# Linear attention and a spectral mix on one core: constants loaded in sixteen pieces, two weight loads cut into row ranges

## The chip, the cores and the metric

The kernel runs on one core of one Trainium2 chip. The metric is device time of one execution in microseconds (us), lower is better. The engines are named as in the profile: PE is TensorE's matmul side and PEld its weight load, DVE is VectorE, ACT is ScalarE, POOL is GpSimd, SP is SyncE. PE, DVE and ACT compute; POOL and SP issue transfers here. Sixteen DMA engines move the data for all of them.

## The reference

```python
# q, k, v: (8, 8, 576, 64) float32: batch, heads, sequence, head width
phi = lambda x: np.where(x > 0, x, np.exp(x) - 1.0) + 1.0
q_p, k_p = phi(q), phi(k)
kv  = einsum('bhsd,bhse->bhde', k_p, v);  z = sum(k_p, axis=2)
num = einsum('bhsd,bhde->bhse', q_p, kv); den = einsum('bhsd,bhd->bhs', q_p, z) + 1e-6
x = (num / den) as (8, 576, 512)          # batch, sequence, heads * width

# w_r, w_i: (64, 512, 512) float32, one complex matrix per mode; w_ch: (512, 512)
X = rfft(x, axis=1)                       # the first 64 modes are used
Y[:, m] = X[:, m] @ (w_r[m] + 1j * w_i[m])   for m < 64, else 0
u = x + irfft(Y, n=576, axis=1)
out = u + maximum(u @ w_ch, 0)            # (8, 576, 512) float32
```

The 64 pairs of matrices w_r and w_i hold 134 MB in float32, and every byte is used once.

## The kernel before

The work has three stages. In the first (to about 112 us) the attention is computed batch by batch, and its first 64 Fourier modes are formed by matmuls with constant cosines and sines (fwd_sb). In the second (to about 388 us) the modes are multiplied by their matrices, two modes at a time: a "pair" p covers modes 2p and 2p + 1, and there are 32 pairs. While they stream, the attention rows are formed a second time, the inverse transform of the modes that are already done is folded into them, and the product with w_ch is made; a plan of work slots spreads this over the pairs. In the third stage the last modes are added and the rows are stored.

The weights of a pair are one tile of 128 partitions by 16 x 512 values in bf16. POOL loads it in two transfers, "half" 0 from w_r into the even partitions and half 1 from w_i into the odd ones (`w_load`, L117). Each transfer has 64 rows of 32 KB in float32 in the source, which arrive as rows of 16 KB in bf16: the transfer converts. Pairs 0 and 1 have a buffer each, pairs 2 to 4 three buffers of their own, and from pair 5 on two buffers are used in turn, so that the load of pair p can be issued when the product of pair p - 2 is finished. The last pair (31) is loaded in smaller pieces by `w_load_last` (L129). Before the stream, POOL also loads w_ch and the small selection constant pick_sb.

`mode_pair(p)` waits for both halves, makes 16 matmuls (`product`, L432), copies the result out of PSUM (`evacuate`, L447 and L449), does the work of its first slot, picks the rows out (`picks`, L455), does its second slot, and runs a number of matmuls that fill time (`keep_warm`, L419). All of these stand in the order written: `pin` keeps every engine's program order, and POOL's transfers among themselves too.

The constants of the inverse transform, inv_sb, are 128 partitions (64 modes, cosine and sine) by 576 values of 2 bytes, 144 KB. SP loads them in one transfer (L541) once the space that they take has been given up by the first stage. They are read first by `row_set` (L628), which makes permuted copies of them in a work slot, and later by the matmuls that add the inverse transform (L683, L745, L752, L760, L893). After inv_sb SP issues nothing until the third stage, in which it sends a copy within the chip (YZ_all, L947) and the stores of the output (L816, L822). The last product of the second stage is y_last (L513), which follows the last pieces of pair 31 one by one.

Completion of transfers is counted in eight counters for POOL's and eight for SP's, used in turn; a transfer whose counter is still in use by the one eight before it waits for that one.

Of the kernel before, what the change touches and what calls it, by code (L numbers as in the profile page):

```python
# [43 lines left out]
def kernel(  # L44
# [10 lines left out]
    nc = tc.nc  # L55
# [3 lines left out]
    NM = moe_w_r.shape[0]  # L59
# [3 lines left out]
    NDW = 4 * NDC  # L63
# [10 lines left out]
    inv_dr = nc.inline_tensor(inv_np, name="dft_inv")  # L74
# [31 lines left out]
    pin = tc.keep_in_program_order  # L106
    PIECES = (slice(0, 2), slice(2, 4), slice(4, 6), slice(6, 7), slice(7, 8))
    HALVES = [slice(0, 64), slice(64, 128)]

    LAST = NM // 2 - 1  # L110

    def w_load(p: int, half: int, pool, tag: str, bufs: int):
        if half == 0:
            w_in[p] = pool.tile([128, NDW, D], BF16, tag=tag, bufs=bufs, name=f"w{p}")
        two = (moe_w_r, moe_w_i)[half][2 * p : 2 * p + 2]
        pin(
            nc.gpsimd.dma_start(  # L117
                out=w_in[p][half::2], in_=two.rearrange("g (r dc) e -> (g r) dc e", dc=NDW)
            )
        )  # L120

    def w_load_last(pool, tag: str, bufs: int):
        w_in[LAST] = pool.tile([128, NDW, D], BF16, tag=tag, bufs=bufs, name=f"w{LAST}")
        for g in range(2):
            for half in range(2):
                rows_in = (moe_w_r, moe_w_i)[half][NM - 2 + g].rearrange("(p dc) e -> p dc e", dc=NDL)
                for dcs in PIECES if (g, half) == (1, 1) else (slice(0, NDL),):
                    dst = w_in[LAST][half::2, g * NDL + dcs.start : g * NDL + dcs.stop]
                    pin(nc.gpsimd.dma_start(out=dst, in_=rows_in[:, dcs, :]))  # L129
# [16 lines left out]
    def w_next():  # L146
        p, half = pending.pop(0)
        pool, tag, bufs = (wpool, "w", W_KEEP) if p < n_keep else (wpre, "wp", W_PRE)
        w_load(p, half, pool, tag, bufs)
# [258 lines left out]
    def w_get(p: int):  # L408
        if p not in w_in and p == LAST:
            w_load_last(wpool, "w", W_KEEP)  # L410
        elif p not in w_in:
            for half in range(2):
                w_load(p, half, wpool, "w", W_KEEP)
        return w_in[p]
# [14 lines left out]
    def product(P, x, n: int, w, dc: int, n_dc: int):  # L429
        c = dc % NDC * 32  # L430
        pin(
            nc.tensor.matmul(  # L432
                P[c : c + n, :], x, w[:, dc, :],
                start=(dc < NDC), stop=(dc >= n_dc - NDC), tile_position=(0, c),
                skip_group_check=True,
            )
        )

    def set_diagonal(p: int):
        for h in range(2):  # L440
            src = xt_v[HALVES[h], :, :, :, p].rearrange("p c t b -> p c (t b)")
            pin(nc.vector.tensor_copy(out=xz[p % 2][HALVES[h], :, h, :], in_=src))  # L442
# [19 lines left out]
    def mode_pair(p: int):  # L462
# [5 lines left out]
        for dc in range(NDW):  # L468
            product(P, xz[p % 2][:, dc].rearrange("p h n -> p (h n)"), 32, w, dc, NDW)
        if p + 1 < LAST:  # L470
            set_diagonal(p + 1)
# [15 lines left out]
    def last_pair():  # L487
        xl = ystage.tile([128, NDL, 2 * B], BF16, name="xl")
        for h in range(2):
            src = xt_v[:, (2 * h + 1) * NDC : (2 * h + 2) * NDC, :, :, LAST]  # L490
            pin(
# [3 lines left out]
            )  # L495
        w = w_get(LAST)
        kk = NM - 2
# [39 lines left out]
    inv_sb = ystage.tile([2 * NM, S], F16, name="inv_sb")  # L537
    inv2_sb = ystage.tile([128, S], F16, name="inv2_sb")
    N_LEAD = 2
    lead_sb = [ystage.tile([128, S], F16, name=f"lead{b}_sb") for b in range(N_LEAD)]  # L540
    nc.sync.dma_start(out=inv_sb, in_=inv_dr.ap())  # L541
    YE_T = ystage.tile([128, NDC, NF, 2 * B], F16, name="YE_T")
    YL = [ystage.tile([128, NDC // 2, 2, 2 * NL, NF // NL, B], F16, name="YL0")]
    Y8 = ystage.tile([128, NDC, NL, 2 * B], F16, name="Y8")
# [44 lines left out]
    def x_of(t: int):  # L589
        if t < B * NJJ:  # L590
            return x_main[t // NJJ][:, t % NJJ, :]
        i = t - B * NJJ
        return x_tail[i // 2][:, i % 2, :]
# [352 lines left out]
    for h, eng in enumerate((nc.sync, nc.gpsimd)):  # L946
        eng.dma_start(  # L947
            out=YZ_all[64 * h : 64 * h + 64 : NF // NL].rearrange("r b z d -> r b (z d)"),
            in_=last.rearrange("p z d -> p (z d)"),
# [15 lines left out]
    def sums_of(n: int, i: int):  # L965
# [8 lines left out]
            out=x_of(0), in0=accs[0][:, 0], scalar=0.0, in1=x_of(0), op0=ALU.max, op1=ALU.add  # L974
# [50 lines left out]
```

## Time and profile before

| | |
|---|---|
| time, median of 3 runs | 421.2 us (421.08 to 421.81) |
| profiled execution: span, first to last instruction | 419.4 us |
| median less that span | 1.8 us |
| busy in the span: PE, DVE, ACT, POOL | 317.2, 231.3, 154.2, 57.4 us |
| moved by the DMA engines | 93.17 MB, mean 222 GB/s |
| of these on the software queue (POOL's) | 12496 packets, 81.48 MB |
| on the hardware queue (SP's) | 4544 packets, 11.22 MB |
| mean granted TensorE clock | 0.830 |

The profile is of one execution, and for that execution it gives the span and no other time; what lies around the span is taken as the 1.8 us between it and the median. Times inside it are counted from the span's start. A line "L432 PE" is an instruction of line 432 of the kernel on PE; "w<-in_moe_w_i_dram" is a transfer into tile w from the input w_i; numbers of buffers are left out of names. A matmul's end is modelled, so a busy PE isn't PE at its peak. In the chain of waits each step is followed by what released the next.

### The profile page before, as it was taken

The numbers are of one execution on the slowest core, as the hardware profiler recorded it, in microseconds if no ns is written. First come the engines' busy times: TensorE is split into PE (matmuls) and PEld (weight loads), VectorE is DVE, ScalarE is ACT, GpSimd is POOL, SyncE is SP. The second block draws the span as 40 slices with busy tenths as digits, with TensorE's granted clock in tenths as the row PEclk, the third lists the DMA queues.
The fourth block names the chain that finished last, engine by engine and source line by source line (L and its number), as shares of the span: only waits on it lengthen the run. The fifth ranks groups of instructions, "written<-read, shape, count | busy, mean of one in ns | idle before, by whom it ended". The sixth has DMA issues, their size and how long they took to land.

```text
span 419.4 us, 7466 instructions
## 1 busy us (share of the span) xinstructions
PE 317.2 (76%) x3143; PEld 164.4 (39%) x3143; DVE 231.3 (55%) x509; ACT 154.2 (37%) x253; POOL 57.4 (14%) x100
## 2 busy tenths in 40 slices
PE   0369998999617875676767686988798877998993
PEld 0257776877301332222222233433343332453421
DVE  4588899785314563463645353464456443522794
ACT  4677798854201011000000233334253432330783
POOL 4222224210011211111111111111111111130000
PEclk9999999579855658665655599899899997899998
DMA  8999999999999999999999999999999999998698
GB/s 217 211 212 216 210 222 203 228 206 223 217 223 208 218 220 209 220 217 212 220 214 213 223 213 214 223 210 216 220 209 219 217 214 219 216 209 166 235 391 328
DMA packets 17073, 93.17 MB, mean 222 GB/s; under 512 B 2112, under 2 KB 3024, under 8 KB 12880
## 3 DMA queue, kind: packets, MB, share of 16 engines
q0 software_dynamic: 12496, 81.48, 93.4%
q1 hardware_dynamic: 4544, 11.22, 7.2%
q8 instruction: 24, 0.39, 0.3%
q14 instruction: 9, 0.07, 0.0%
HBM read 163.93 MB, written 9.44 MB: 413 GB/s over the span
## 4 chain that ended last, share of the span: by engine, by line
DMA 64%; PE 23%; DVE 4%; POOL 3%; ACT 3%; issue 2%; DVEq 0%; ACTq 0%; POOLq 0%
DMA w<-in_moe_w_i_dram 53%; DMA pick_sb<-row_pick 8%; PE P L432 6%; DMA k<-in_k_dram 3%; PE acc L760 3%; PE kvp L257 3%; PE acc L800 2%; POOL w L117 2%; PE z L726 1%; DVE x L293 1%; ACT ke L208 1%; PE xf L355 1%; PE zl L419 1%; PE qTp L237 1%; PE num L163 1%
## 5 line engine op out<-in xcount | busy, mean ns | idle before, releaser
L432 PE MATMUL P<-w,xz 128*32 128x512 bf16 x496 | 42.6, 475 | 37.6 <-DMA w<-in_moe_w_i_dram 35.4
L419 PE MATMUL zl<-wch,id 128*128 128x512 f16 x185 | 58.2, 466 | 0.0
L449 ACT CAST ys<-P 128x512 f16<-128x512 f32 x15 | 8.8, 586 | 132.4 <-PE P L432 132.4
L117 POOL DMA_DIRECT2D w<-in_moe_w_r_dram x31 | 17.3, 559 | 246.4 <-PE P L432 211.8
L447 DVE CAST ys<-P 128x512 f16<-128x512 f32 x17 | 11.8, 692 | 51.0 <-PE P L432 51.0
L706 PE MATMUL eps<-wch,xTw 128*128 128x512 f16 x144 | 39.3, 399 | 0.0
L432 PEld LDWEIGHTS <-xz 128*32 128x32 bf16 x496 | 12.6, 108 | 63.3 <-DMA w<-in_moe_w_i_dram 40.3
L163 PEld LDWEIGHTS <-qT 64*128 64x128 f16 (+1 forms) x640 | 22.6, 122 | 29.6 <-issue 15.6
L689 ACT CAST x16w<-x_main 128x512 f16<-128x512 f32 x32 | 19.8, 618 | 37.8 <-DVE x_main L687 37.8
L687 DVE TENSOR_TENSOR x_main<-ya,x_main 128x512 f32<-128x512 f32 x32 | 22.0, 689 | 16.5 <-PE ya L683 16.3
L257 PE MATMUL kvp<-vpad,ke 32*128 32x130 f16 x576 | 24.3, 263 | 8.9 <-ACT qT L244 6.1
L442 DVE COPY xz<-xt_c 64x256 bf16<-64x256 bf16 x62 | 23.0, 371 | 10.9 <-PE P L432 10.0
L419 PEld LDWEIGHTS <-id 128*128 128x128 f16 x185 | 18.9, 112 | 25.6 <-issue 14.3
L714 ACT CAST E<-eps 128x512 f16<-128x512 f32 (+1 forms) x40 | 21.2, 540 | 17.7 <-PE eps L706 17.7
L257 PEld LDWEIGHTS <-ke 32*128 32x128 f16 x576 | 22.3, 116 | 10.6 <-issue 8.6
L163 PE MATMUL nw<-kv_sb,qT 64*128 64x65 f16 (+1 forms) x320 | 18.2, 231 | 9.8 <-DVE x_tail L650 4.7
L237 PE MATMUL qTp<-id,qe 128*128 128x128 f16 x144 | 15.1, 289 | 10.6 <-DVE qe L221 9.5
L293 DVE TENSOR_TENSOR x<-num,rd 128x512 f16<-128x512 f32 x32 | 22.1, 692 | 1.1
L650 DVE TENSOR_TENSOR x_main<-nw,rd 128x256 f32<-128x256 f32 x32 | 11.2, 416 | 18.8 <-PE nw L163 18.8
L455 PE MATMUL yt<-pick_sb,ys 128*128 128x32 f16 (+1 forms) x128 | 8.8, 185 | 16.7 <-DMA pick_sb<-row_pick 9.4
L698 DVE COPY xTw<-xTp 128x512 f16<-128x512 f16 x36 | 15.0, 416 | 10.3 <-PE xTp L696 10.3
L208 ACT ACTIVATE qe<-q 128x1152 f16<-128x1152 f16 (+1 forms) x16 | 17.9, 1157 | 7.2 <-DMA q<-in_q_dram 7.1
(118 smaller groups left out, 507.5 us busy)
## 6 DMA issues: line engine op xcount, KB each, us to landing
w<-in_moe_w_r_dram POOLq DMA_DIRECT2D x31, 1024.0 KB, 13.2
w<-in_moe_w_i_dram POOLq DMA_DIRECT2D x31, 1024.0 KB, 17.5
out_dram<-x_main SPq DMA_DIRECT2D x12, 512.0 KB, 3.6
k<-in_k_dram POOLq DMA_DIRECT2D x8, 576.0 KB, 12.9
v<-in_v_dram POOLq DMA_DIRECT2D x8, 576.0 KB, 14.3
q<-in_q_dram POOLq DMA_DIRECT2D x7, 576.0 KB, 12.6
out_dram<-x_main SPq DMA_DIRECT2D x8, 256.0 KB, 4.0
q<-in_q_dram SPq DMA_DIRECT2D x2, 576.0 KB, 4.5
```

The costliest lines, as they stand in the source:

```text
L117: nc.gpsimd.dma_start(out=w_in[p][half::2], in_=two.rearrange("g (r dc) e -> (g r) dc e", dc=NDW))
L163: mm = nc.tensor.matmul(num[hpo][orow, c0 : c0 + 65], qT[rows, hpp, h2, cols], kv_sb[rows, hpp, h2, :])
L208: pin(nc.scalar.activation(out=ev[:, c], in_=heads(nm, b, c), func=AF.Exp))
L257: nc.tensor.matmul(kv_ps[:, h2, 0:130], phi["k", b][r0 : r0 + 32, j // NJ, j % NJ].rearrange("p o d -> p (o d)"), vp[r0 : r0 + 32, :, j, 0 ...
L293: nc.vector.tensor_tensor(out=dst.rearrange("p (o c d) -> p o c d", o=2, c=4), in0=nv[:, :, :, 0:64], in1=rden.unsqueeze(3).broadcast_to([ ...
L419: pin(nc.tensor.matmul(last_ps[0], id16, wch16[:, 0, :]))
L432: nc.tensor.matmul(P[c : c + n, :], x, w[:, dc, :], start=(dc < NDC), stop=(dc >= n_dc - NDC), tile_position=(0, c), skip_group_check=True,)
L442: pin(nc.vector.tensor_copy(out=xz[p % 2][HALVES[h], :, h, :], in_=src))
L687: pin(nc.vector.tensor_tensor(out=x, in0=acc, in1=x, op=ALU.add))
L689: pin(nc.scalar.copy(out=x16w[t], in_=x))
L706: nc.tensor.matmul(e_ps, xT[:, c, :], wch16[:, c, :], start=(c == 0), stop=(c == NDC - 1))
L714: pin(nc.scalar.copy(out=dst, in_=e_ps[:, cols]))
```

## The change

The single load of inv_sb becomes sixteen loads of eight partitions each, on the same queue and at the same place. The load of pair 12's half 0 becomes three transfers, of rows 0 to 47, 48 to 55 and 56 to 63. That of pair 20's half 0 becomes two, of rows 0 to 59 and 60 to 63. They stand at the same place in POOL's order, one behind the other. Every other transfer, and all work on PE, DVE and ACT, keeps its order. Where PE waited for one count of inv_sb it now waits for all eight of SP's counters, and for the two divided weights it waits for two counts and one count more. All later transfers use other counters in turn.

```diff
     LAST = NM // 2 - 1
+    SPLIT = {(12, 0): (0, 48, 56, 64), (20, 0): (0, 60, 64)}
 
     def w_load(p: int, half: int, pool, tag: str, bufs: int):
...
         two = (moe_w_r, moe_w_i)[half][2 * p : 2 * p + 2]
-        pin(
-            nc.gpsimd.dma_start(
-                out=w_in[p][half::2], in_=two.rearrange("g (r dc) e -> (g r) dc e", dc=NDW)
-            )
-        )
+        rows_in = two.rearrange("g (r dc) e -> (g r) dc e", dc=NDW)
+        cuts = SPLIT.get((p, half), (0, 64))
+        for r0, r1 in zip(cuts, cuts[1:]):
+            pin(
+                nc.gpsimd.dma_start(
+                    out=w_in[p][half + 2 * r0 : half + 2 * r1 - 1 : 2], in_=rows_in[r0:r1]
+                )
+            )
...
-    nc.sync.dma_start(out=inv_sb, in_=inv_dr.ap())
+    for r0 in range(0, 2 * NM, 8):
+        nc.sync.dma_start(out=inv_sb[r0 : r0 + 8], in_=inv_dr.ap()[r0 : r0 + 8])
```

## The prediction

> **What bounds the kernel now.** I read the page first, for the share of the transfers and for the queues.
>
> ```profile
> span 419.4 us, 7466 instructions
> ...
> DMA  8999999999999999999999999999999999998698
> ...
> q0 software_dynamic: 12496, 81.48, 93.4%
> q1 hardware_dynamic: 4544, 11.22, 7.2%
> q8 instruction: 24, 0.39, 0.3%
> ```
>
> The transfers are busy in every slice up to the last few, and nearly all of it is the software queue, which POOL feeds with the weights (q0). The hardware queue q1 is SP's: it carries the constants and, at the end, the stores. q8 brings TensorE its instructions, 24 packets of 16 KB. Next the chain of work that ended last, in order of time, over two weight pairs and over the end of the stream:
>
> ```profile
> 329.49 1.08 PE P L432 x16
> 330.86 0.54 POOL w L117
> 331.40 17.46 DMA w<-in_moe_w_i_dram
> 348.90 1.07 PE P L432 x16
> ...
> 370.81 2.16 POOL w L129 x4
> 372.98 13.65 DMA w<-in_moe_w_i_dram
> 386.67 0.36 PE y_last L513 x8
> ```
>
> TensorE waits for a landing, multiplies for 1.1 us, and POOL issues the pair after next. A transfer takes 17.5 us from issue to landing because the other buffer's pair is queued ahead of it, so the queue doesn't run dry. At the end the last weight piece lands, y_last follows, and everything after it hangs on that landing. The transfers' view of 200 to 300 us shows how full the queue is:
>
> ```profile
> q0 software_dynamic: 1639, 21.48, 101.0%
> q8 instruction: 4, 0.07, 0.2%
> ...
> w<-in_moe_w_r_dram POOLq DMA_DIRECT2D x10, 1024.0 KB, 13.2
> w<-in_moe_w_i_dram POOLq DMA_DIRECT2D x10, 1024.0 KB, 17.5
> ```
>
> Twenty transfers of 64 rows take 97 us (two pairs per 19.4 us in the chain), 4.85 us each. A row is one packet of 16 KB (1024 KB over 64 rows), so each of the 16 engines carries four, 1.21 us a row. The bound is therefore not the mean engine but the one that finishes last. The trace has that: every transfer is reported by 16 counts, one per engine. Their times after the first of them, in us:
>
> ```
> landed  23.5: 0 .04 .07 .08 .10 .12 .14 .17 .19 .21 .23 .27 .28 .30 .33 .34
> landed 116.8: 0 .15 .19 .23 .24 .29 .33 .85 1.16 1.19 1.21 1.29 1.45 2.40 2.44 2.58
> landed 387.9: 0 .02 .07 .11 .17 .18 .47 2.18 2.34 3.11 3.14 3.18 3.25 3.31 3.32 3.34
> ```
>
> The engines start level and drift apart. The cause can be read from q8's packets: their durations repeat with period eight (893, 893, 948, 945, 935, 975, 975, 962 ns), so eight engines carry the instruction fetches in turn, three each by the end, 3 x 0.95 = 2.8 us. That is the group at 3.1 to 3.3 us (seven engines; the eighth has had two by then). One more engine is at 2.2 to 2.3, and seven are early. The mean of the last row is 1.76, so perfect balance would be worth 3.34 - 1.76 = 1.6 us, no more. Nothing in the profile names an engine's number.
>
> **The change, part by part.** The bytes are the same; what changes is which engine carries them.
>
> The constants. The view of tile inv_sb:
>
> ```profile
> L628 PE MATMUL rows<-inv_sb,row_sel x6: 203/422/608, 155.5 to 157.3; 128*128 128x512 f16 x3, 128*128 128x64 f16 x3
> ...
> L541 SPq DMA_DIRECT2D inv_sb<-dft_inv x1: 320/320/320, 111.2 to 111.2; - x1
> ...
> DMA to landing us min/median/max: 10.8/10.8/10.8
> ```
>
> SP issues sixteen times in place of once, 16 x 0.32 = 5.1 us, with nothing behind it until the first store at 391 us. Now 128 packets of 1152 bytes lie eight to an engine, 64 ns each. A piece of eight partitions has eight such packets, so it reaches at most eight engines. If all pieces take the same eight, these carry 16 rows in place of 8 (8 x 64 = 0.51 us) and 15 more completion counts (9 to 22 ns each in the trace, 0.14 to 0.33 us): +0.65 to +0.84, while the other eight lose 0.51. If the pieces rotate, it is nothing. I take +0.65. The landing: the rows are served between 16 KB rows of the other queue, so 16 rows and 16 counts take at most 32 x 1.21 = 39 us, until 150 or 151 us; the first use is at 155.5 us, which covers it. If the cover were gone, TensorE would stand before L628, while POOL's next weight issue that needs TensorE comes at 164.8 us; so up to some 9 us more are free. By the Trainium skill ("DMA: Bandwidth & Descriptors", "Rules for kernel authors"), small transfers should be gathered, since under 64 KB one pays mostly overhead. Its fit of 2.0 us a transfer would make sixteen in a row an estimated 32 us against one load's 10.8 measured here, still ahead of 155.5 us and worth nothing in the sum.
>
> The weight of pair 12 (lands near 197 us) in 48, 8 and 8 rows. POOL issues twice more, 2 x 0.54 = 1.1 us, ahead of the pair's second half; that half waits behind a whole pair, 9.7 us, so it is hidden. 48 rows are three to an engine. The two eights are one row on each of eight engines: if they take different eights, every engine is back at four and the price is nothing; if they take the same eight, those carry five (+1.21 us) and the others three (-1.21). The trace before has no transfer on fewer than 16 engines, so both ends stay; I take nothing: every transfer that the trace does show is level over the engines, and two eights served in turn would be level too.
>
> The weight of pair 20 (near 276 us) in 60 and 4. Sixty whole rows do not divide by 16: four to each of 15 engines leave one without. The four rows then fall on four engines; at most one of these is the empty one, and at least three carry five: +1.21 us. If the 60 lie as 4 and 3 and the 4 rows fill the gaps, it is nothing. I take +1.21: filling the gaps needs a planner, and a fixed order gives a surplus. Of the engines only seven are early, so in three or four neighbours a late one is likely.
>
> The waits that come with it are a few more counts for TensorE and POOL (51 ns for one such wait at L628), all long met when they are asked for. The tail after the last landing, 387.9 to 419.4, is untouched.
>
> The Trainium skill's rule for this ("DMA: Bandwidth & Descriptors", "Why a DMA increments its semaphore by 16 and not by 1") is that a transfer spreads over the largest number up to 16 that divides the outermost dimension, on SP's path always over the lowest-numbered engines, on POOL's over consecutive ones from a cursor that moves on, or in some direct copies over the first engines with the rows rounded up. By the cursor the estimate would be 0 for the eights and 1.21 us for 60 and 4; by the rounding, 2.4 us for both; no run here yet shows either.
>
> The sum: a late engine at 3.34 us takes 0.65 (constants) and 1.21 (pair 20), and nothing else: +1.86 us at the last landing. Nothing behind can take it up, as y_last and the stores chase that landing. A row added at 276 us stays to the end, because an engine that is behind has a queue ahead of it all the time. The span goes from 419.4 to 421.3; the median lies 1.8 us above this span, so 421.2 + 1.86 = 423.1.
>
> **Rivals.** First, both eights hit the same engines: another 1.21, 3.07 in all, 424.3 us. For it: a fixed mapping would also put all sixteen constant pieces on the same eight. Against: nothing seen.
>
> Second, the change is not what it looks like: rows are cut finer and spread over all 16, or the pieces rotate and level out. Then a level split costs some counts of 22 ns, and the time is 421.2 to 421.9 (with the constants' 0.65 alone).
>
> Third, faster: the extra rows fall on the early engines, and the late ones are relieved. Late engines would lose 0.51 + 1.21 = 1.72 and end at 1.6; early ones gain up to 0.65 + 1.21 and end at 2.3. That is 1.0 us earlier, 420.2; with rows of 60 and 4 also on the right side, at best the 1.6 us of perfect balance, 419.6. Against it stands a count: an eight-row piece needs eight engines and only seven are early, so the eighth starts at 2.2 at least and would end at 4.0, later than 3.34. It decides only if this eighth engine is also the one that the 60 rows leave out (3 to 4 rows, 3.6 to 4.8 us). The early engines and the eighth must be the right eight; if the fetches' eight are scattered, it fails.
>
> **How the numbers follow.** About 0.2%, 0.84 us, is what a measurement here can tell from no change. Forecast (one row and the constants on a late engine) 0.40; both rows 0.22; nothing or the constants alone 0.15; faster 0.23, since I know no engine's number. Slower is 0.40 + 0.22 = 0.62. The forecast's and first rival's own range is 422.4 (one row, no constants) to 424.5 (0.84 and two rows: 3.3). The whole range reaches down to 420.1, just under the third rival's 420.2; below it and above 424.5 I leave about 0.16.
>
> **What would show it.** Right: the last weight landing moves from 387.9 to about 389.7; the 16 counts of the last transfer spread over 5.2 us in place of 3.34, with a step of 0.65 after the constants and 1.21 after pair 20; L628's rows still start near 155 us; the stretch after the last landing stays 31.5 us. Wrong: the spread shrinks and the landing comes earlier (third rival); the spread steps by 1.21 already after pair 12 (first); the spread stays 3.3 (second); or TensorE is seen waiting for inv_sb.

## The result and the profile after

| | before | after |
|---|---|---|
| median of the shared comparison (4 runs each) | 421.35 us (421.08 to 421.81) | 423.28 us (422.86 to 423.54) |
| ratio after to before, 95% interval | | 1.0045 (1.0031 to 1.0059) |
| profiled execution: span | 419.4 us | 421.1 us |
| last weight landing | 387.88 us | 389.58 us |
| span after that landing | 31.5 us | 31.5 us |

The changed kernel is slower by 1.93 us between the medians. The prediction was 423.1, between 420.1 and 424.5. The page of the profile after, first line, transfer row of the slices, and queues (packets, MB, share of 16 engines):

```profile
span 421.1 us, 7495 instructions
...
DMA  8999999999999999999999999999999999997698
...
q0 software_dynamic: 12576, 81.48, 93.1%
q1 hardware_dynamic: 4656, 11.23, 7.2%
q8 instruction: 24, 0.39, 0.3%
```

The bytes are the same. What is added is packets: 112 on q1 and 80 on q0. The 112 give the width of a piece of the constants: the single load has 16 completion counts, sixteen pieces of k counts have 16k, and 16k - 16 = 112 makes k = 8. So each piece used eight engines. The 80 on q0 are all packets of 4 bytes, the size of a count. Three added transfers at 16 counts make 48; the other 32 are as many as the rows that the cut pieces lack to a multiple of 16 (8 + 8 + 12 + 4). So every piece on this queue seems to be laid out for all sixteen engines, with a filler where a row is missing.

The chain of waits, 325 to 395 us (start, length, what):

```profile
333.08 17.46 DMA w<-in_moe_w_i_dram
350.55 0.04 issue
350.59 1.08 PE P L436 x16
...
371.37 2.14 POOL w L133 x4
373.50 14.78 DMA w<-in_moe_w_i_dram
388.28 0.05 issue
388.32 0.36 PE y_last L517 x8
```

It is the same chain as before, with the same 17.46 us from issue to landing in the middle of the stream. The last product follows its landing and starts at 388.32 us in place of 386.67. The stretch behind the last landing, from the table by stage (length; busy PE, PEld, DVE, ACT, POOL; TensorE clock; share and GB/s of the transfers):

```profile
389.60:421.10 31.50, 24.11 (x135) 7.97 (x133) 23.35 (x25) 20.06 (x38) 0.57 (x1) 0.95 0.83 318
```

31.5 us again. The 1.7 us were lost before the last landing, in a stream that is busy in every slice. The times of the 16 counts show where. They are given in us after the first of the 16, for three transfers; "half 0 of 13" is one transfer after pair 12's second half:

```
                        last at  others after the first
before, half 0 of 13     207.05  0 .02 .08 .08 .14 .15 .17 1.26 1.69 2.04 2.06 2.11 2.13 2.24 2.24 2.27
after,  half 0 of 13     208.52  0 .14 1.14 2.20 2.23 2.27 2.35 2.54 3.31 3.32 3.34 3.75 3.88 5.03 5.41 5.50
before, last of stream   387.88  0 .02 .07 .11 .17 .18 .47 2.18 2.34 3.11 3.14 3.18 3.25 3.31 3.32 3.34
after,  last of stream   389.58  0 .05 .60 .67 .76 .77 .90 .96 1.05 1.05 1.83 2.23 2.67 3.78 3.88 4.07
```

After pair 12 the spread has more than doubled, 2.27 to 5.50 us, and the last engine is 1.47 us later than before: that is the first rival's sign. At the end of the stream the spread has shrunk to 4.07 us but the last engine is still 1.70 us late. On an engine a packet starts when the one before it there has ended, so packets can be chained by their times. Chained through pair 12, eight engines carry 3, 1 and 1 rows of the three transfers and the other eight 3, 0 and 0. Both eights fell on the same eight engines.

### The profile page after: what moved, and what is told of

The parts are those of the page before. It is cut to its first block, busy times and chain, and to the rows that moved or that the text cites. A ratio compares the mean times of both kernels' runs of the same rounds, so it can differ in the third digit from the quotient of the medians.

```text
span 421.1 us, 7495 instructions
## 1 busy us (share of the span) xinstructions
PE 314.8 (75%) x3143; PEld 162.1 (38%) x3143; DVE 230.6 (55%) x509; ACT 153.9 (37%) x253; POOL 59.0 (14%) x103
## 4 chain that ended last, share of the span: by engine, by line
DMA 67%; PE 20%; DVE 4%; issue 3%; POOL 3%; ACT 2%; DVEq 0%; ACTq 0%; POOLq 0%
DMA w<-in_moe_w_i_dram 52%; DMA pick_sb<-row_pick 8%; DMA k<-in_k_dram 7%; PE P L436 7%; PE acc L765 3%; PE acc L805 2%; POOL w L121 2%; PE kvp L261 1%; PE eps L711 1%; ACT ke L212 1%; PE zl L423 1%; PE ya L688 1%; DVE x L297 1%; PE xTp L701 1%; POOL w L133 1%
## 5 line engine op out<-in xcount | busy, mean ns | idle before, releaser
L436 PE MATMUL P<-w,xz 128*32 128x512 bf16 x496 | 45.7, 505 | 38.4 <-DMA w<-in_moe_w_i_dram 36.1
L121 POOL DMA_DIRECT2D w<-in_moe_w_r_dram x34 | 18.5, 546 | 243.3 <-PE P L436 209.5
L446 DVE COPY xz<-xt_c 64x256 bf16<-64x256 bf16 x62 | 23.1, 372 | 12.6 <-PE P L436 11.7
L261 PE MATMUL kvp<-vpad,ke 32*128 32x130 f16 x576 | 22.6, 251 | 8.9 <-ACT qT L248 6.1
L261 PEld LDWEIGHTS <-ke 32*128 32x128 f16 x576 | 20.7, 110 | 10.5 <-issue 8.3
## 6 DMA issues: line engine op xcount, KB each, us to landing
w<-in_moe_w_r_dram POOLq DMA_DIRECT2D x29, 1024.0 KB, 13.2
```

What stands on the lines that cost most here:

```text
L121: nc.gpsimd.dma_start(out=w_in[p][half + 2 * r0 : half + 2 * r1 - 1 : 2], in_=rows_in[r0:r1])
L261: nc.tensor.matmul(kv_ps[:, h2, 0:130], phi["k", b][r0 : r0 + 32, j // NJ, j % NJ].rearrange("p o d -> p (o d)"), vp[r0 : r0 + 32, :, j, 0 ...
L436: nc.tensor.matmul(P[c : c + n, :], x, w[:, dc, :], start=(dc < NDC), stop=(dc >= n_dc - NDC), tile_position=(0, c), skip_group_check=True,)
```

## The experiments

**The theory** after seeing this: the cost is rows on engines. Both eights of pair 12 fall on one set of eight engines that contains late ones, and their extra row of 1.21 us stays to the end; the constants add a little on such a set; the 60 and 4 add little or much. **The rivals**: the cost is per transfer (18 added transfers, 1.93 us, 0.107 us each), wherever the rows go; or it is as the prediction's sum had it, with pair 20 paying and pair 12 free. All runs are compared with the kernel before on the same chip; "d" below is the difference of the medians. The ratio is worked out on its own and isn't the quotient of the medians: with four eights it stands for 2.66 us (2.1 to 3.2) where d is 3.05. The edits are against the changed kernel.

| run | d, us | ratio (95% interval) | last engine after half 0 of 13, to before | last landing, to before |
|---|---|---|---|---|
| constants alone | +0.47 | 1.0009 (1.0000 to 1.0018) | +0.44 | +0.55 |
| pair 12 alone | +1.31 | 1.0032 (1.0019 to 1.0044) | +1.42 | +1.41 |
| pair 20 alone | -0.01 | 1.0000 (0.9991 to 1.0009) | +0.17 | +0.20 |
| level cuts | +0.21 | 1.0005 (0.9996 to 1.0014) | +0.28 | +0.32 |
| pair 12, four eights | +3.05 | 1.0063 (1.0050 to 1.0077) | +2.76 | +3.42 |
| eights at pair 28 | +1.05 | 1.0022 (1.0013 to 1.0031) | +0.06 | +1.14 |
| pair 12, four fours | +3.05 | 1.0072 (1.0060 to 1.0085) | +3.61 | +3.19 |
| half rows, four fours | +0.42 | 1.0011 (1.0002 to 1.0020) | +1.29 | +0.76 |
| constants and pair 12 | +1.66 | 1.0043 (1.0030 to 1.0055) | +1.51 | +1.50 |
| both weights | +1.50 | 1.0040 (1.0026 to 1.0054) | +1.46 | +1.47 |
| the whole again | +2.03 | 1.0047 (1.0035 to 1.0060) | +1.74 | +2.21 |

The two right columns are of one profiled execution each, against the one of before. The last of them follows the times within 0.4 us in every run: the landing of the last weight sets the time.

### The parts alone

Constants alone:

```diff
-    SPLIT = {(12, 0): (0, 48, 56, 64), (20, 0): (0, 60, 64)}
+    SPLIT = {}
```

> Only the sixteen constant loads; both weight loads whole. Slowest-engine account: each piece reports eight counts with its data, so eight engines carry 16 rows in place of 8; if one of the late engines is among them, the last weight landing moves by about 0.65 us and the time is about 422.0; if the late ones are all on the other side, it falls by up to 0.5, about 420.9. Cost-per-transfer account (18 added transfers cost 1.93 us, 0.107 us each, wherever their rows lie): 15 added transfers, +1.6 us, about 422.9.

Pair 12 alone:

```diff
-    SPLIT = {(12, 0): (0, 48, 56, 64), (20, 0): (0, 60, 64)}
+    SPLIT = {(12, 0): (0, 48, 56, 64)}
...
-    for r0 in range(0, 2 * NM, 8):
-        nc.sync.dma_start(out=inv_sb[r0 : r0 + 8], in_=inv_dr.ap()[r0 : r0 + 8])
+    nc.sync.dma_start(out=inv_sb, in_=inv_dr.ap())
```

> Only pair 12 in 48, 8 and 8 rows. Slowest-engine account: in the changed kernel's trace both eights are on the same eight engines (five rows there, three on the others), so with a late engine among the eight the last landing moves by 1.21 us, about 422.5; with none it comes up to 1.21 earlier, about 420.3. Account of the prediction's own term (the eights level out): 421.35, no change. Cost-per-transfer account: two transfers, +0.2 us, about 421.6.

Pair 20 alone: the same with `SPLIT = {(20, 0): (0, 60, 64)}`.

> Only pair 20 in 60 and 4 rows. Slowest-engine account: four engines carry five rows, eleven carry four, one carries none; +1.21 us and about 422.5 if one of the four is among the latest, less (down to 0) where it is one of the middle; the engine with none runs ahead by 4.8 us and then runs dry, so it gives nothing. Cost-per-transfer account: one transfer, +0.1 us, about 421.5.

The constants cost 0.47 us and pair 12 alone 1.31; pair 20 alone costs nothing. The chain of waits of the kernel with pair 12 alone, end of the stream:

```profile
370.87 1.01 PE P L436 x16
...
372.17 2.13 POOL w L133 x4
374.30 13.71 DMA w<-in_moe_w_i_dram
...
388.06 0.36 PE y_last L517 x8
```

The same view with pair 20 alone:

```profile
369.41 1.01 PE P L436 x16
...
370.70 2.16 POOL w L133 x4
372.86 13.99 DMA w<-in_moe_w_i_dram
...
386.89 0.36 PE y_last L517 x8
```

y_last starts 1.39 us later than before's 386.67 in the one, 0.22 in the other. That refutes the sum in which pair 20 pays 1.21 and pair 12 nothing. It speaks against a price per transfer too: the two transfers added at pair 12 cost 1.31 us, the fifteen of the constants 0.47, the one of pair 20 nothing.

### As many transfers, but level

Each of these pieces has 16, 32 or a multiple of 16 rows, so that no engine gains a row on another; eleven transfers are added.

```diff
-    SPLIT = {(12, 0): (0, 48, 56, 64), (20, 0): (0, 60, 64)}
+    SPLIT = {(12, 0): (0, 16, 32, 48, 64), (20, 0): (0, 32, 64)}
...
-    for r0 in range(0, 2 * NM, 8):
-        nc.sync.dma_start(out=inv_sb[r0 : r0 + 8], in_=inv_dr.ap()[r0 : r0 + 8])
+    for r0 in range(0, 2 * NM, 16):
+        nc.sync.dma_start(out=inv_sb[r0 : r0 + 16], in_=inv_dr.ap()[r0 : r0 + 16])
```

> Cuts that leave every engine with what it had: the constants in eight loads of 16 partitions, pair 12 in four times 16 rows, pair 20 in two times 32: 11 added transfers. Slowest-engine account: no engine carries a row more, so 421.35 within 0.3 us, and the spread of the last transfer's counts stays at 3.3 us. Cost-per-transfer account: 11 x 0.107, +1.2 us, about 422.5.

Measured +0.21 us, interval -0.17 to +0.59 (0.9996 and 1.0014 of 421.5). A price of 0.107 us each would be 1.18. Counting transfers is refuted; where their rows fall decides. Nor is it POOL's time to issue, as pair 12 has one piece more here than in the changed kernel. After half 0 of pair 13 the counts spread 2.65 us, against 2.27 in before and 5.50 in the changed kernel. The end of the chain:

```profile
371.08 2.66 POOL w L133 x5
373.74 13.80 DMA w<-in_moe_w_i_dram
387.54 0.05 issue
387.59 0.36 PE y_last L517 x8
```

### Are they always the same engines?

Two more eights in the same pair. If eights were served in turn, four of them would be level again (two rows on each of 16 engines); if they always take the same eight, these carry two rows more. The constants stay in one load here and in the next three kernels.

```diff
-    SPLIT = {(12, 0): (0, 48, 56, 64), (20, 0): (0, 60, 64)}
+    SPLIT = {(12, 0): (0, 32, 40, 48, 56, 64)}
```

> Pair 12 in 32 rows and four times 8 rows, nothing else changed. Slowest-engine account: the eights always fall on the same eight engines, which then carry six rows in place of four, two rows of 1.21 us more; against 421.55 before that is 424.0. If the eights alternate between the halves, 421.55; if each added transfer costs what one did in the kernel with 48, 8 and 8 (1.31 us for two), four cost 2.6, which is hard to tell from two rows, but then the kernels with level cuts and with fours must cost as much.

Measured +3.05 us by the medians and 2.66 by the ratio (2.1 to 3.2), against the 2.45 expected. The counts one transfer after pair 12 fall into two eights:

```
last at 209.81: 0 .09 1.04 2.00 2.05 2.06 2.14 2.29 | 4.44 4.50 4.53 4.80 5.17 6.36 6.62 6.87
```

The hit set carried 2 + 4 rows and the other 2, four rows or 4.84 us apart. Taking 4.84 off the right eight gives -.40 to 2.03 with five early engines and three late ones; the left eight has five late ones. So all four eights took one set, and that set holds early and late engines. The last engine is 2.76 us later than before, near 2 x 1.21. The chain ends in the landing as before:

```profile
374.85 2.70 POOL w L133 x5
377.54 13.12 DMA w<-in_moe_w_i_dram
390.66 0.04 issue
390.71 0.36 PE y_last L517 x8
```

The same eights at another place, to see whether the set or the price depends on it:

```diff
-    SPLIT = {(12, 0): (0, 48, 56, 64), (20, 0): (0, 60, 64)}
+    SPLIT = {(28, 0): (0, 48, 56, 64)}
```

> The cut into 48, 8 and 8 made at pair 28 in place of pair 12, nothing else changed. Slowest-engine account: an engine that is last has rows queued all the time, so a row is worth the same wherever it is added: +1.2 to 1.3 us, about 422.8. If a row added early is partly made up later, more than the 1.31 of pair 12.

Measured +1.05 us. Nothing differs one transfer after pair 12 (+0.06); one transfer after pair 28's second half the last engine is 1.10 us late and it ends 1.14 late. So the row is paid in about the same size sixteen pairs later.

On the way from pair 12 to the end the lag isn't constant, though. At half 0 of pairs 13, 17 and at the end the last engine is later than before by 1.42, 0.35 and 1.41 us with pair 12 alone, by 2.76, 1.70 and 3.42 with four eights, and by 1.47, 0.41 and 1.69 in the changed kernel. The fall at pair 17 comes from before: an instruction packet starts there at 244.3 us, and its spread goes from 2.32 us at pair 16 to 3.33 at pair 17. How much of a row is seen at one moment depends on which engines such packets have reached by then; what it costs is read at the last landing.

### Fewer engines, and a try for a gain

Four fours in place of two eights. If the four engines are early ones, the late engines lose a row and the stream could end earlier; if one of them is late, it carries three rows more.

```diff
-    SPLIT = {(12, 0): (0, 48, 56, 64), (20, 0): (0, 60, 64)}
+    SPLIT = {(12, 0): (0, 48, 52, 56, 60, 64)}
```

> Pair 12 in 48 rows and four times 4 rows, nothing else changed. Slowest-engine account: the fours fall on the same four engines, which carry seven rows, 3.63 us more, and the other twelve three. In the trace of the kernel with 60 and 4 alone the four were early engines (0 to 0.5 us after the first); they end near 4.0 and the rest near 2.1, so the last landing moves from 3.34 to about 4.0: +0.6 us, 422.1. If the four are late ones: 3.3 + 3.6, about 425.2. If the fours move on by four engines each time they level out: 421.55.

The expectation was wrong: +3.05 us. The counts one transfer after pair 12:

```
last at 210.66: 0 .15 .24 .32 1.47 2.26 2.37 2.38 2.44 2.46 2.55 2.71 | 4.91 5.11 5.43 6.63
```

The four on the right carried seven rows and the twelve others three. Less 4.84 they stand at .07, .27, .59 and 1.79: three early ones and one that stands closer to the late ones (the expectation had taken all four for early). That one is 3.61 us later than before's last, 3 x 1.21 = 3.63. Here the chain of waits doesn't show the landing in front of y_last:

```profile
383.02 0.70 DVE ys L451
...
384.04 2.17 PE zl L423 x10
...
389.06 0.66 PE zl L423 x3
389.72 0.48 PE y_last L517 x16
```

TensorE's own work fills the stretch up to 389.72 us, and then 16 products follow in one go: the pieces of the last pair arrive close together. The last landing is 3.19 us later than before, and the time 3.05.

Then half the load (SPLIT is empty, and each transfer takes the columns d0 to d1 of its rows): 48 rows whole, the first half of the columns of rows 48 to 63 in one transfer, and the other half in four transfers of four rows. The four engines carry 1.5 rows more and the twelve others 0.5 less.

```diff
-        for r0, r1 in zip(cuts, cuts[1:]):
+        parts = [(r0, r1, 0, NDW) for r0, r1 in zip(cuts, cuts[1:])]
+        if (p, half) == (12, 0):
+            h = NDW // 2
+            parts = [(0, 48, 0, NDW), (48, 64, 0, h)] + [(r, r + 4, h, NDW) for r in range(48, 64, 4)]
+        for r0, r1, d0, d1 in parts:
...
-                    out=w_in[p][half + 2 * r0 : half + 2 * r1 - 1 : 2], in_=rows_in[r0:r1]
+                    out=w_in[p][half + 2 * r0 : half + 2 * r1 - 1 : 2, d0:d1], in_=rows_in[r0:r1, d0:d1]
```

> Made to gain: in pair 12, 48 whole rows, then the first half of the columns of the last 16 rows over all engines, then their second half in four transfers of 4 rows. Slowest-engine account: four early engines carry 5.5 rows in place of 4 (+1.8 us, to about 2.3), the other twelve 3.5 (-0.6 us, 3.34 to 2.74): the last landing 0.6 us earlier, about 420.95. Cost-per-transfer account: five added transfers, +0.5 us or more.

It was expected to gain and it lost 0.42 us. One transfer after pair 12 the first count comes 0.72 us earlier than before and the last 1.29 later: the twelve lost their half row (0.6), and the late one of the four gained 1.5 (1.8 us, from 1.79 to 3.6, against a last of 2.27 before). No kernel of the study was faster than before by more than the noise.

### Pairs of parts, and the whole

`SPLIT = {(12, 0): (0, 48, 56, 64)}` with the constants in eights:

> The constants in sixteen loads and pair 12 in 48, 8 and 8; pair 20 whole. If the parts add as measured alone (0.47 and 1.31 us over 421.5), 423.3, and pair 20 is worth nothing in the whole change either. If pair 20's row falls on an engine that the other two have already made one of the last, as the step of 0.8 us at pair 20 in the changed kernel's trace suggests, this is up to 0.8 below the whole, about 422.5 to 422.8.

Both weights as changed, the constants in one load:

> Both weights cut as in the change, the constants in one load. If the parts add as measured alone (1.31 and 0), 422.8. If one late engine gets a row at pair 12 and another at pair 20, 421.5 + 2.4 = 423.9. If the late one of pair 20's four is among pair 12's eight but starts 1 us before the last, the second row shows only in part: 422.9 to 423.2.

The changed kernel once more, on the same chip as these two:

> The changed kernel itself beside the two above, for an interval on one chip: 423.3, 1.7 to 2.0 us over the kernel before.

Measured +1.66, +1.50 and +2.03. The parts alone add up to 0.47 + 1.31 - 0.01 = 1.77. Pair 20 adds 0.37 to constants and pair 12 together (2.03 - 1.66) and 0.19 to pair 12 alone (1.50 - 1.31); neither is beyond what the intervals allow, which are about 0.5 us either way.

## Why the prediction was right, and where it was not

The time and the direction were right, and so was the outline: the stream is bound by the last engine, an added row on a late engine is paid at the last landing, and the tail behind it is untouched. The sum itself was right by luck, through two errors that cancel: of 0.65 + 0 + 1.21 the runs show 0.47, 1.31 and 0 to 0.4.

**Constants, right in size.** Taken at +0.65, measured +0.47, interval 0 to 0.76. Each piece had eight data counts, so the same eight engines may carry all sixteen rows. The step didn't show when the pieces were served but when an instruction packet came to such an engine: in the kernel with the constants alone the spread is 2.24 us at pair 7, then an instruction packet comes at 157.5 us, and the spread is 3.73 at pair 8 and 3.03 at pair 11. In before, the packet of the same place (158.1 us, 893 ns in both) left it at 2.22 and 2.27. In two executions in which the instruction packets begin elsewhere in their cycle (974 ns) the spread is wider as soon as the pieces have been served: 2.99 us at pair 5 with constants and pair 12, 3.15 in the second profiled execution of the changed kernel, against 2.58 with pair 12 alone and the same first packet. With the constants alone the last engine is 0.25 us earlier than before at pair 17 and 0.55 later at the end. That a surplus row on a late engine makes the 0.47 us is therefore argued, not shown.

**The constants' issue and cover: one size wrong, the cover right.** SP's timeline of the changed kernel, against the 5.1 us that the prediction gave for sixteen issues:

```profile
109.08 13.20 SPq L546 DMA_DIRECT2D inv_sb<-dft_inv  x16
```

13.2 us: there are eight completion counters and sixteen loads, so from the ninth on each waits for the one eight before it, which the prediction's own step left out. The counters show it: the first eight are issued by 111.9 us, the last count of the first comes at 115.1, and the ninth is issued at 115.6. The instructions of tile inv_sb:

```profile
L546 SPq DMA_DIRECT2D inv_sb<-dft_inv x16: 263/293/343, 109.1 to 122.0; - x16
...
L633 PE MATMUL rows<-inv_sb,row_sel x6: 190/284/389, 155.0 to 156.5; 128*128 128x512 f16 x3, 128*128 128x64 f16 x3
```

The last count came at 135.3 us, where one load had landed at 122.1; that is 26.2 us from the start of the first issue, against the 32 us that the prediction had estimated for sixteen in a row. The bound was 150 or 151 us and the first use still starts at 155.0. So the cover held, and nothing waited.

**Pair 12, the step that failed.** "Two eights served in turn would be level too": they aren't served in turn. Within each kernel every small piece fell on the same set: two eights in the changed kernel, four eights, four fours. The first rival had this mechanism, at 1.21 us; measured is 1.31. By the Trainium skill ("DMA: Bandwidth & Descriptors", "Why a DMA increments its semaphore by 16 and not by 1") the software queue's cursor would move on from one such transfer to the next, and pair 12 would be free. The same section's exception, rows rounded up over sixteen engines from the first on, fits what these converting loads show: 32 fillers, and one set for all small pieces. The page gives it for some direct copies without saying which, and that the set is the first engines isn't shown, as the profile names none. The prediction had set its price beside the sum at 2.4 us for both weights; the runs give 1.50.

POOL's issues were as predicted, 1.1 us more and hidden:

```profile
185.26 1.55 POOL L121 DMA_DIRECT2D w<-in_moe_w_r_dram  x3 [9.53 <-PE P L436]
186.80 0.57 POOL L121 DMA_DIRECT2D w<-in_moe_w_i_dram  x1
```

The transfers' view of 180 to 215 us confirms that the queue stayed full over the cut, at 101.5%, with 11.7 and 12.7 us from issue to landing:

```profile
q0 software_dynamic: 626, 7.54, 101.5%
...
w<-in_moe_w_r_dram POOLq DMA_DIRECT2D x1, 768.0 KB, 11.7
w<-in_moe_w_r_dram POOLq DMA_DIRECT2D x2, 128.0 KB, 12.7
```

**Pair 20, the other step that failed.** Taken at +1.21, it cost nothing alone. The distribution was as worked out: eleven engines carry 4 and 0 rows, four carry 4 and 1, one carries none. "In three or four neighbours a late one is likely" was true as well, as the four fours of pair 12 show, if the set is the same. What was wrong is that such an engine isn't the last one. Alone, the last engine at pair 20 is 0.14 us later than before and 0.10 earlier one pair on: a late engine that is a row ahead of the last can take a row without being seen. The counts fit this. Before the cut (half 1 of pair 19) seven engines stand within 0.56 us of the first, one at 1.89, and the last at 3.97. Of the seven, one is then left out, three keep their places and three are 1.2 us later; the fourth extra row fits the engine at 1.89, which it leaves about 0.6 us ahead of the last. No engine can be followed by name, so this stays a reading. With the other parts in, more is seen for a while: in the changed kernel the last engine's lag to before goes from +0.40 at pair 19 to +1.20 at pair 21, and to +1.69 at pair 22, behind the instruction packet at 289.0 us. With pair 12 alone it goes from +0.35 to +1.35 over the same packet. So most of pair 20's shift is covered again by the engine which that packet delays.

**The spread.** Predicted 5.2 us at the end, measured 4.07. It had been 5.50 after pair 12 and shrank from the early side: the first count of the last transfer comes 0.97 us later than before. As a sign it isn't firm: in the second profiled execution of the same kernel the last transfer spreads 2.57 us. The reading is that an early engine runs dry when it is far ahead, because the transfers behind it wait for buffers that the late engines hold; that they wait for buffers is argued. The engine that the 60 rows left out shows it best: at pair 20 the first count is 3.6 us earlier than before, and one pair on 0.27 later (with pair 20 alone 4.28 earlier, then 1.84). The prediction had the last engine's queue never empty, which nothing here contradicts; it had no word on the others'.

**The signs.** Landing at 389.7 predicted, 389.58 measured. L633 near 155: 155.0. Tail 31.5: 31.5. The step after pair 12 was named as the sign of the first rival, and it is there. The second rival (all spread level) had the spread stay at 3.3 us and the time at 421.9 or less; neither came.

**The third rival** (a gain) fell by its own count: an eight-row set needs eight early engines, and this one holds three late ones. A gain remains open for a way to put rows on the early engines alone, which cutting rows didn't give here.

## What to carry to other kernels

Where a stream of transfers is full, look at the completion counts one by one: the landing belongs to the last engine, and a transfer whose rows don't divide evenly over sixteen added its surplus to one fixed set here. Cut in multiples of sixteen rows: eleven transfers more cost 0.21 us (within the interval of nothing), while two pieces of eight rows cost 1.31. A surplus row cost about its own time once at both places tried for two eights (pairs 12 and 28); it is paid only if the engine that gets it is the last or becomes so.

## What the runs showed of the hardware

- The instruction fetches of TensorE, 24 packets of 16 KB that take 0.89 to 0.98 us each in before up to its last landing, are the cause argued for the drift between the engines of before. Their cycle of eight durations starts at another point from one execution to the next (first packets 936 ns in before, 974 with pair 12 alone, 893 with pair 20 alone, 948 with the level cuts). It does so for one program too: the two profiled executions of the changed kernel start at 935 and 974 ns. So which engine is late by how much can differ between executions.
- Pieces of eight and of four rows on the software queue took the same eight and the same four engines within each kernel that had several of them, and a load of 60 rows left one engine without a row. Each row missing to a multiple of sixteen shows as one more 4-byte packet: 16 with two eights, 32 with four eights, 48 with four fours, 16 with 60 and 4, none with level cuts.
- Overload on some engines makes others run dry: with four eights and with four fours at pair 12, the first count of the last transfer came 3.40 and 3.81 us later than before, nearly as late as the last one (3.42 and 3.19). From 205 to 225 us the DMA engines moved 208 and 205 GB/s in these two kernels, against 215 before, and from 225 to 260 us 210 and 209 against 216.
